# Splitting and distributing the q and k halves of a sparse-attention kernel: where GpSimd writes them, and how many transfers carry the rest

## The chip, the cores and the metric

The program runs on one core of a Trainium2 chip (trn2). The metric is the device time of one execution in microseconds (us). A core has five engines, each with an instruction stream of its own: TensorE (PE, matmuls and transposes; its weight loads are listed as PEld), VectorE (DVE), ScalarE (ACT), GpSimd (POOL) and SyncE (SP, which issues nearly all transfers here). They meet only at semaphores. The core has 16 DMA engines.

## What is computed

Three layers follow each other: attention that keeps only scores within tau of a row's maximum, a top-1 mixture of 8 experts, and a SwiGLU layer. The change lies in the attention.

```python
batch, n_heads, seq, head_dim = (2, 8, 576, 64)
def _attn_ref(q, k, v, tau):
    scores = (1.0 / np.sqrt(q.shape[-1])) * np.matmul(q, k.transpose(0, 1, 3, 2))
    thresh = np.max(scores, axis=-1, keepdims=True) - tau
    scores = np.where(scores >= thresh, scores, -1000000000.0)
    attn = np.exp(scores - np.max(scores, axis=-1, keepdims=True))
    attn = attn / (np.sum(attn, axis=-1, keepdims=True) + 1e-09)
    return np.matmul(attn, v)
def reference(...):            # x: (1152, 512), capacity 288
    x = attn_out.transpose(0, 2, 1, 3).reshape(1152, 512)
    x = _moe_ref(x, w_gate, w1, w2, capacity)   # argmax expert, relu(x w1) w2, times its gate
    return (silu(x @ w_gate2) * (x @ w_val)) @ w_out
```

## The kernel before

**Units.** The 8 heads are taken in 4 pairs (`hp`), the 576 rows of a batch as 4 blocks of 128 and a tail of 64. A pair has 9 units: 4 blocks of batch 0, 4 of batch 1, and one unit (`st` 8) for the tails of both batches. So there are 36 units, numbered 0 to 35; pair `hp` begins at unit 9 hp. In one unit and for each of the two heads (`j`), TensorE computes 128 x 576 scores (`emit_qk`, L597, tile `s`), VectorE takes the maximum (L607) and later masks (L631), ScalarE exponentiates (L620), and TensorE transposes the unit before (L653), which ScalarE copies out (L657, tile `pT`).

**Halves.** The products must be as exact as float32, so q and k are split into a rounded half and the rest (`hi`, `lo`). The tile `KP` holds for one head, on 128 partitions, both halves of k: one in partitions 0 to 63, the other in 64 to 127. The q tiles (`QH`, `QL`; buffers `qhl` for odd pairs, `ring[3]` and `ring[4]` for even ones) hold each half of q twice, in both partition halves. `QT` does the same for the tail rows of q.

**Staging.** For pair 0 the halves are made in another way. For pairs 1 to 3 `stage_tasks(hp + 1)` makes them while pair `hp` is computed; its five tasks go into the list `trq` at the end of unit `st == TST`, and up to two are taken per unit. A task transposes a 128 x 512 block of both heads on TensorE (`turn`, L515), ScalarE copies it to the scratch buffer `sraw` (L528, L530), GpSimd makes the rounded half and the rest into `ring[1]` or `ring[0]` (`parts`, L508 and L510, on all 128 partitions), and SP issues the transfers that carry each half of each head to its partitions: 4 per block of k (L537), 4 per block of q (L540), 4 for the tails of k (L559), and one unit after the pair has begun 8 for the tails of q (`qtails`, L568). Tasks run in the order k of batch 0, q of batch 0, tails, k of batch 1, q of batch 1.

**Values.** `pv_tasks` multiplies the masked weights with v in groups of two units: for each of four row chunks and both heads a matmul with a 128 x 64 weight (L675), and for the 64 tail rows one with a 64 x 64 weight (L678). A group's work waits in the list `pvq`. In each unit a loop with a budget (`credit`) takes from `pvq`, `trq` and `xl` (the 128 x 144 product that follows, L709); from `st >= UST` on, staging goes ahead of values.

**Queues.** TensorE, ScalarE, VectorE and GpSimd run in the order in which the code is written; SP's order is made by a scheduler. In the built program every SP transfer also waits on one of eight DMA semaphores that go round, so that it follows the landing of the transfer eight places ahead of it. `load_qkv` (L333, L336, L348) loads a pair's q, k and v from HBM, `late_consts` fills the token tables.

Of the kernel before, what the change touches and what calls it, by code (L numbers as in the profile page):

```python
# [10 lines left out]
F32 = mybir.dt.float32  # L11
# [11 lines left out]
def attention_moe_swiglu_kernel(  # L23
# [62 lines left out]
    TST = 4  # L86
    QST = 1
    FB = 1800
# [5 lines left out]
    UST = 5  # L94
# [222 lines left out]
    idw = ld.tile([128, KD, 128 + 2 * NE], F32, name="idw")  # L317

    def load_qkv(hp):
        h0 = 2 * hp  # L320
        r = raw[hp] = {}
        srcs = {"k": (k, 1), "q": (q, 1), "v": (v, 2)}
        for nm, (src, nb) in srcs.items():
            if hp and nm != "v":
                r[nm] = ld.tile([128, B, C4, 2, D], F32, tag=nm, name=nm, bufs=nb)
            else:
                r[nm] = ld.tile([128, B, 2, C4, D], F32, tag=nm, name=nm, bufs=nb)
            r[nm + "t"] = ld.tile([128, 2, D], F32, tag=nm + "t", name=nm + "t", bufs=nb)
# [24 lines left out]
        main("k", 1, nc.sync)  # L353
        main("q", 1, nc.sync)
        tail("q", nc.sync)
        for b in range(B):
            main("v", b, nc.sync)
        tail("v", nc.sync)
# [42 lines left out]
    QT = [ld.tile([128, 2, 2 * 128], F32R, name=f"qt{j}") for j in range(2)]  # L401
    QTH, QTL = [[QT[j][:, w] for j in range(2)] for w in range(2)]
    traw = ld.tile([128, 2, 128], F32, name="traw")
    thl = ld.tile([128, 2, 2, 128], F32R, name="thl")
    qhl = [ld.tile([128, 2, B * SM], F32R, name=f"qhl{j}") for j in range(2)]
    ready = set()

    def tr_qk_tasks(hp):
# [6 lines left out]
        def ensure(j):  # L415
            if (hp, j) not in KP:
                KP[hp, j] = qk.tile([128, B, S], F32R, tag=f"kp{j}", name=f"kp{j}")
                QH[hp, j], QL[hp, j] = qhl[j][:, 0], qhl[j][:, 1]
                if hp % 2 == 0:
                    QH[hp, j], QL[hp, j] = ring[3 + j][:, 0], ring[3 + j][:, 1]  # L420
# [14 lines left out]
        def qmain(b, j, w):  # L435
            def f():
                ps = mp.tile([128, 512], F32R, tag="m", name="ps_q")
                tr(ps, [fl(raw[hp]["qh" if w == 0 else "ql"][:, b, j, c]) for c in range(C4)])
                dst = (QH, QL)[w][hp, j][:, b * SM:(b + 1) * SM]
# [53 lines left out]
    def stage_tasks(hp):  # L493
        kx, qx = ring[1], ring[0]
# [3 lines left out]
        def ensure():  # L498
            if (hp, 0) in KP:
                return  # L500
            for j in range(2):
                KP[hp, j] = qk.tile([128, B, S], F32R, tag=f"kp{j}", name=f"kp{j}")
                QH[hp, j], QL[hp, j] = qhl[j][:, 0], qhl[j][:, 1]
                if hp % 2 == 0:
                    QH[hp, j], QL[hp, j] = ring[3 + j][:, 0], ring[3 + j][:, 1]

        def parts(dst, src):
            nc.gpsimd.tensor_scalar(out=dst[0], in0=src, scalar1=1.0, scalar2=1.0,  # L508
                                    op0=ALU.mult, op1=ALU.mult)
            nc.gpsimd.tensor_tensor(out=dst[1], in0=src, in1=f32(dst[0]), op=ALU.subtract)  # L510
# [7 lines left out]
        def main(nm, b):  # L518
            def f():
# [4 lines left out]
                x, dst = (kx, sraw[:, 1, cs]) if nm == "k" else (qx, sraw[:, 0, cs])  # L524

                def ev():
# [4 lines left out]
                    parts([x[:, i, cs] for i in range(2)], dst)  # L531
                    for j in range(2):
                        for i in range(2):
                            to, frm = slice(i * D, (i + 1) * D), slice(j * D, (j + 1) * D)
                            if nm == "k":
                                o = ST if j else 0
                                nc.sync.dma_start(f32(KP[hp, j][to, b, o:o + SM]), f32(x[frm, i, cs]))  # L537
                            else:
                                t = ring[3 + j] if hp % 2 == 0 else qhl[j]
                                nc.sync.dma_start(f32(t[to, :, cs]), f32(x[frm, :, cs]))  # L540
# [5 lines left out]
        def tails():  # L546
# [3 lines left out]
            def ev():  # L550
                nc.scalar.copy(traw[:, 0], ps[:, 0:128])
                nc.scalar.activation(out=traw[:, 1], in_=ps[:, 128:256], func=ACTF.Identity,
                                     scale=kfac[:, 0:1])
                parts([thl[:, i] for i in range(2)], traw)
                for j in range(2):
                    o = 0 if j else SM
                    frm = slice(j * D, (j + 1) * D)
                    for i in range(2):
                        nc.sync.dma_start(  # L559
                            f32(KP[hp, j][i * D:(i + 1) * D, :, o:o + ST]),  # L560
                            f32(thl[frm, i, 1]).rearrange("p (b t) -> p b t", b=B))
            return ev, None

        def qtails():
            for j in range(2):
                for i in range(2):
                    for w in range(2):
                        nc.sync.dma_start(  # L568
                            f32(QT[j][i * D:(i + 1) * D, w]).rearrange(
                                "p (x t) -> p x t", t=ST)[:, 0:4:3, :],  # L570
                            f32(thl[j * D:(j + 1) * D, w, 0]).rearrange("p (b t) -> p b t", b=B))
# [13 lines left out]
    def emit_qk(i):  # L585
# [4 lines left out]
        col = (b * C4 + c) * 128  # L590
        if b >= 0:
            jobs = [(QH[hp, j][:, col:col + 128], b), (QL[hp, j][:, col:col + 128], b)]
# [69 lines left out]
    def pv_tasks(g):  # L662
# [5 lines left out]
        def item(bb, o, w, c, last):  # L668
            def f():
# [3 lines left out]
                for j in range(2):  # L673
# [104 lines left out]
    keep_warm(mp, WARM0, 128)  # L778
    nc.scalar.dma_start(tau_sb, tau.partition_broadcast(128))
# [82 lines left out]
    for u in range(NU):  # L862
        hp, st = divmod(u, 9)
        live, tpos = u < NU, 0 <= u - 1 < NU
        if u == 5:
            late_consts()
# [70 lines left out]
        if live and hp and st == QST:  # L937
            qtails()
    assert not trq
# [134 lines left out]
    olo = [rp.tile([128, 128], BF16, name=f"olo{t}") for t in range(NTL)]  # L1074
# [482 lines left out]
```

## Time and profile before

| | us |
|---|---|
| median of 3 runs (561.7 to 566.77) | 564.54 |
| the profiled execution: its time | 564.97 |
| its span, from the first instruction to the last | 563.3 |
| attention, about | 10 to 172 |
| mean granted TensorE clock, share of full speed | 0.986 |

The page's 40 slices show TensorE busy in almost every slice, 95% of the span. That is a share over stages with different limits, and a matmul that waits inside its pipeline counts as busy, so a stage is read from the starts of its units and from the waits, which the section on the rows shows.

### The profile page before, as it was taken

Reading aid. Unit: us, or ns where it says so; the run is one execution under the profiler, and the core shown is the slowest. Engines: PE = TensorE matmul, PEld = TensorE weight load, DVE = VectorE, ACT = ScalarE, POOL = GpSimd, SP = SyncE. Lnnn points to the kernel's source line nnn. Section 1 sums busy time; section 2 is a strip of 40 time slices with the busy share of each in tenths; the row PEclk is TensorE's granted clock in tenths of the full one; section 3 lists DMA queues with packets and bytes.
Section 4 is the critical chain, followed back from the end, with each engine's and each line's share of the span. In section 5 each row is a group of like instructions: output and inputs, shape, how many; then the busy total and the mean of one; then the engine's idle time right before and its main releaser. Section 6 shows DMA issues by size and latency. Waiting matters only on the chain. (4 is left out here: it accounts for less than half of the span.)

```text
span 563.3 us, 9844 instructions
## 1 busy us (share of the span) xinstructions
PE 536.4 (95%) x3600; PEld 481.0 (85%) x3602; DVE 409.7 (73%) x825; ACT 295.2 (52%) x573; POOL 85.4 (15%) x145
## 2 busy tenths in 40 slices
PE   7999988999997799999999999999999999999996
PEld 6787866877773799998998889999999999888884
DVE  5988876888876399989988977888896748722220
ACT  4977664676651399877866743334332333332321
POOL 6541050055452500000000000000000000011101
PEclk8999998999999799999999999999999999999999
DMA  7557467457301888977666442442341300000001
GB/s 185 173 150 171 118 143 172 110 140 205 116 29 35 313 289 281 328 224 232 224 219 223 151 149 81 145 149 83 143 149 76 112 40 1 0 38 37 20 38 42
DMA packets 67895, 77.94 MB, mean 138 GB/s; under 512 B 25216, under 2 KB 43136, under 8 KB 67840
## 3 DMA queue, kind: packets, MB, share of 16 engines
q1 hardware_dynamic: 66256, 72.52, 42.4%
q0 software_dynamic: 1440, 4.72, 2.2%
q8 instruction: 30, 0.49, 0.3%
q14 instruction: 25, 0.20, 0.1%
q10 hardware_dynamic: 144, 0.00, 0.0%
HBM read 61.89 MB, written 4.72 MB: 118 GB/s over the span
## 5 line engine op out<-in xcount | busy, mean ns | idle before, releaser
L1460 PE MATMUL pgv<-yT,ring 128*128 128x384 f32 x828 | 145.1, 337 | 0.0
L1460 PEld LDWEIGHTS pgv<-yT,ring 128*128 128x128 f32 x828 | 144.9, 188 | 0.0
L210 ACT CAST ring<-raw 128x1024 fp32r<-128x1024 f32 x57 | 60.8, 1066 | 51.2 <-DVE raw L238 49.5
L657 ACT COPY pT<-ps_pt 128x512 f32<-128x512 f32 (+1 forms) x108 | 52.3, 486 | 41.6 <-PE ps_pt L653 41.6
L607 DVE TENSOR_REDUCE nm<-s 128x1 f32<-128x576 f32 x72 | 54.4, 755 | 17.2 <-PE s L597 17.1
L631 DVE SCALAR_TENSOR_TENSOR e<-s,th,e 128x576 f32<-128x576 f32 x72 | 58.7, 816 | 6.2 <-ACT e L620 4.9
L1513 POOL DMA_INDIRECT out_dram<-ob,ids x9 | 8.7, 972 | 358.9 <-ACT ob L1512 351.7
L620 ACT ACTIVATE e<-s,nm 128x576 f32<-128x576 f32 x72 | 54.3, 754 | 2.2 <-DVE nm L607 1.8
L288 DVE TENSOR_TENSOR ring<-raw,ring 128x1024 fp32r<-128x1024 f32 x44 | 53.3, 1218 | 0.0
L1231 PE MATMUL ps_y<-h,ring 128*128 128x448 f32 (+3 forms) x160 | 48.8, 370 | 3.6 <-DVE h L1358 3.4
L214 DVE TENSOR_TENSOR hs<-h,hs 128x768 fp32r<-128x768 f32 x18 | 17.2, 958 | 48.1 <-ACT hs L210 48.1
L653 PE MATMUL ps_pt<-ident,e 128*128 128x128 f32 x324 | 47.9, 276 | 0.0
L1231 PE MATMUL ps_h<-xw,ring 128*128 128x448 f32 (+3 forms) x160 | 46.4, 362 | 0.0
L1508 PE MATMUL po<-ring,hs 128*128 128x512 f32 x108 | 42.0, 389 | 0.0
L1507 PE MATMUL po<-ring,hs 128*128 128x512 f32 x108 | 42.0, 389 | 0.0
L1509 PE MATMUL po<-ring,hs 128*128 128x512 f32 x108 | 42.0, 389 | 0.0
L1232 PE MATMUL ps_y<-h,ring 128*128 128x224 f32 (+3 forms) x160 | 40.0, 250 | 0.0
L1232 PE MATMUL ps_h<-xw,ring 128*128 128x224 f32 (+3 forms) x160 | 40.0, 250 | 0.0
L675 PE MATMUL ps_pv<-pT,v 128*64 128x256 f32 (+2 forms) x400 | 39.9, 331 | 0.0
L653 PEld LDWEIGHTS ps_pt<-ident,e 128*128 128x128 f32 x324 | 39.7, 142 | 0.2 <-issue 0.2
L1231 PEld LDWEIGHTS ps_y<-h,ring 128*128 128x128 f32 x160 | 30.0, 188 | 8.3 <-DVE h L1358 7.4
L1480 ACT ACTIVATE sg<-pgv 128x384 f32<-128x384 f32 x36 | 17.5, 486 | 28.4 <-PE pgv L1460 18.9
(224 smaller groups left out, 975.9 us busy)
## 6 DMA issues: line engine op xcount, KB each, us to landing
raw<-in_moe_w_dram SPq DMA_DIRECT2D x25, 1024.0 KB, 5.1
rawx<-in_moe_w_dram SPq DMA_DIRECT2D x7, 1024.0 KB, 5.9
raw<-in_moe_w_gate_dram SPq DMA_DIRECT2D x6, 1024.0 KB, 5.0
qhl<-ring SPq DMA_DIRECT2D x16, 256.0 KB, 4.4
raw<-in_moe_w_out_dram SPq DMA_DIRECT2D x4, 1024.0 KB, 4.9
kp<-ring SPq DMA_DIRECT2D x24, 128.0 KB, 2.3
rawx<-in_moe_w_val_dram SPq DMA_DIRECT2D x3, 1024.0 KB, 5.0
raw<-in_moe_w_val_dram SPq DMA_DIRECT2D x3, 1024.0 KB, 5.0
```

What stands on the lines that cost most here:

```text
L210: nc.scalar.copy(dst, src)
L288: lo_eng.tensor_tensor(out=lo_, in0=src, in1=f32(hi_), op=ALU.subtract)
L607: nc.vector.tensor_reduce(out=nm_t[u][:, j:j + 1], in_=s_t[i][:, :, 0:SH], axis=AX.XY, op=ALU.max, negate=True)
L620: nc.scalar.activation(out=e_t[u][:, j].rearrange("p (a s) -> p a s", a=2), in_=s_t[i][:, :, 0:SH], func=ACTF.Exp, bias=nm_t[u][:, j:j + 1 ...
L631: nc.vector.scalar_tensor_tensor(out=ev, in0=s_t.pop(i)[:, :, 0:SH], scalar=th_t[u][:, j:j + 1], in1=ev, op0=ALU.is_ge, op1=ALU.mult, accu ...
L653: nc.tensor.transpose(ps[:, c * 128:(c + 1) * 128], ef[:, (c0 + c) * 128:(c0 + c + 1) * 128], ident)
L657: return lambda: nc.scalar.copy(pT[g][:, c0:c0 + m, o:o + 128], ps[:, 0:m * 128].rearrange("p (c t) -> p c t", c=m))
L1231: mm(ps[:, 0:2 * W], ws(wp, 0), x[:, 0:2 * W], start=first, stop=False)
L1232: mm(ps[:, 0:W], ws(wp, 1), x[:, 0:W], start=False, stop=last)
L1460: mm(ps[:, 0:TH], (gw, vw)[w][:, i, kk, fl * 128:(fl + 1) * 128], yT[:, x, kk, th * TH:(th + 1) * TH], start=i + x + kk == 0, stop=i == 1 ...
L1507: mm(po, hs[:, 0, fl], ws[:, 0, sl], start=f == 0, stop=False)
L1508: mm(po, hs[:, 0, fl], ws[:, 1, sl], start=False, stop=False)
```

## The change

- GpSimd writes one half of each split straight into the tile where it belongs: for k, the rounded half of head 0 into `KP` (partitions 0 to 63) and the rest of head 1 into `KP` (64 to 127); the two other halves go through `ring[1]` and one transfer each. For q both halves are written in place and one transfer per head copies them to the other partitions. Each GpSimd instruction covers 64 partitions instead of 128, so there are twice as many.
- By the order that the built programs print, a pair needs 30 SP transfers where it needed 50 (the rows of one pair, its loads and its results counted; the note on the change says 52).
- The order of tasks is k, tails, q for batch 0, then k and q of batch 1; `TST` goes from 4 to 3 and `UST` from 5 to 4.
- The tails of v lie in two fixed tiles `vtail`, zeroed at the start, one 128-row weight per head: its own 64 rows, zeros in the other 64.
- From pair 2 on v is loaded at `st == VST` (5) of the pair before, not with q and k; `late_consts` runs at unit 11, not 5; `olo` takes the space of an `e` buffer.

```diff
-    TST = 4
+    TST = 3
     QST = 1
+    VST = 5
...
-    UST = 5
+    UST = 4
...
+    vtail = [ld.tile([128, B, 2, D], F32, name=f"vtail{i}") for i in range(2)]
...
             if hp and nm != "v":
-                for h in range(2):
-                    eng.dma_start(r[nm][:, b, :, h],
-                                  srcs[nm][0][b, h0 + h, 0:SM, :].rearrange("(p c) d -> p c d", c=C4))
+                eng.dma_start(r[nm][:, b],
+                              srcs[nm][0][b, h0:h0 + 2, 0:SM, :].rearrange(
+                                  "h (p c) d -> p c h d", c=C4))
...
-                eng.dma_start(r[nm + "t"][i * ST:(i + 1) * ST], src_t)
+                dst = r[nm + "t"][i * ST:(i + 1) * ST]
+                eng.dma_start(dst[:, :, i] if nm == "v" else dst, src_t)
...
-                    parts([x[:, i, cs] for i in range(2)], dst)
-                    for j in range(2):
-                        for i in range(2):
...
-                                nc.sync.dma_start(f32(KP[hp, j][to, b, o:o + SM]), f32(x[frm, i, cs]))
...
-                                nc.sync.dma_start(f32(t[to, :, cs]), f32(x[frm, :, cs]))
+                    lo_, up = slice(0, D), slice(D, 2 * D)
+                    if nm == "k":
+                        k0, k1 = [KP[hp, j][:, b, o:o + SM] for j, o in ((0, 0), (1, ST))]
+                        x = kx[:, cs]
+                        rounded(k0[lo_], dst[lo_])
+                        rest_of(x[lo_], dst[lo_], k0[lo_])
+                        nc.sync.dma_start(f32(k0[up]), f32(x[lo_]))
+                        rounded(x[up], dst[up])
+                        rest_of(k1[up], dst[up], x[up])
+                        nc.sync.dma_start(f32(k1[lo_]), f32(x[up]))
+                    else:
+                        for j, frm, to in ((0, lo_, up), (1, up, lo_)):
+                            t = by_batch(ring[3 + j] if hp % 2 == 0 else qhl[j])[:, b]
+                            rounded(t[frm, 0:SM], dst[frm])
+                            rest_of(t[frm, SM:2 * SM], dst[frm], t[frm, 0:SM])
+                            nc.sync.dma_start(f32(t[to]), f32(t[frm]))
...
-        return [main("k", 0), main("q", 0), tails, main("k", 1), main("q", 1)], qtails
+        return [main("k", 0), tails, main("q", 0), main("k", 1), main("q", 1)], qtails
...
-                        mm(ps[j * D:(j + 1) * D, o:o + w], r["vt"][j * ST:(j + 1) * ST, bb, :],
-                           p[j * ST:(j + 1) * ST, C4, o:o + w], start=False, stop=True)
+                        mm(ps[j * D:(j + 1) * D, o:o + w], r["vt"][:, bb, j, :],
+                           p[:, C4, o:o + w], start=False, stop=True)
...
+    for vz in vtail:
+        nc.vector.memset(vz, 0.0)
...
-        if u == 5:
+        if u == 11:
             late_consts()
...
+        if live and st == VST and hp + 1 in vlate:
+            assert not any(g[0] < hp for _, _, g in pvq)
+            vlate.pop(hp + 1)()
```

The order of the built programs shows three places. SP, staging of pair 2 (during pair 1), before: the transfers of the first block of k (`kp<-ring`), of q (`ring_98`, `ring_99`), results of pair 0 (`xd<-xr`), the tails of k (`kp<-thl`), then the second block of k.

```order
L748 DMA xd<-xr 128x3x128
L537 DMA kp_1118<-ring_96 64x512 x2
L537 DMA kp_1119<-ring_96 64x512 x2
L540 DMA ring_98<-ring_95 64x2x512 x2
L540 DMA ring_99<-ring_95 64x2x512 x2
L748 DMA xd<-xr 128x128
L748 DMA xd<-xr 128x2x128
L559 DMA kp_1118<-thl 64x2x64 x2
L559 DMA kp_1119<-thl 64x2x64 x2
```

The same place of the change:

```order
L557 DMA kp_1063<-ring_96 64x512
L560 DMA kp_1064<-ring_96 64x512
L586 DMA kp_1063<-kth 64x2x64
L589 DMA kp_1064<-kth 64x2x64
L775 DMA xd<-xr 128x128
L775 DMA xd<-xr 128x2x128
L337 DMA k<-in_k_dram 128x8x64
L566 DMA ring_98<-ring_98 64x1024
L566 DMA ring_99<-ring_99 64x1024
```

The tails of k now stand third and fourth and not eleventh to fourteenth, and six transfers carry what twelve did. One load for pair 3 (`k<-in_k_dram`) now stands among them.

GpSimd, the same staging, before: the first block of k (`ring_96`), a logit sum (`lg`) in between, the first block of q (`ring_95`) and the tails (`thl`).

```order
L508 TENSOR_SCALAR ring_96<-raw_103 128x512
L510 TENSOR_TENSOR ring_96<-raw_103,ring_96 128x512
L508 TENSOR_SCALAR ring_95<-raw_103 128x512
L510 TENSOR_TENSOR ring_95<-raw_103,ring_95 128x512
L729 TENSOR_TENSOR lg<-lt 128x24
L508 TENSOR_SCALAR thl<-traw 128x256
L510 TENSOR_TENSOR thl<-traw,thl 128x256
```

The same place of the change, up to where the first block of q begins (it has four such instructions too, into `ring_98` and `ring_99`):

```order
L526 TENSOR_SCALAR kp_1063<-raw_103 64x512
L530 TENSOR_TENSOR ring_96<-raw_103,kp_1063 64x512
L526 TENSOR_SCALAR ring_96<-raw_103 64x512
L530 TENSOR_TENSOR kp_1064<-raw_103,ring_96 64x512
L526 TENSOR_SCALAR kp_1063<-traw 64x2x64
L530 TENSOR_TENSOR kth<-traw,kp_1063 64x128
L526 TENSOR_SCALAR kth<-traw 64x128
L530 TENSOR_TENSOR kp_1064<-traw,kth 64x2x64
L526 TENSOR_SCALAR thl<-traw 128x128
L530 TENSOR_TENSOR thl<-traw,thl 128x128
L756 TENSOR_TENSOR lg<-lt 128x24
```

Ahead of the last result of q's first block there were four instructions on 512 columns; now there are eight of these, and six on the tails.

TensorE, end of one unit and the next two, in pair 1, before: `ps_pv<-pT,v` are value matmuls with a 128-row weight, `ps_pv<-pT,vt` those with a 64-row weight, the rest are scores and transposes.

```order
L678 MATMUL ps_pv<-pT,vt 64x256 x2
L675 MATMUL ps_pv<-pT,v 64x64 x8
L678 MATMUL ps_pv<-pT,vt 64x64 x2
L675 MATMUL ps_pv<-pT,v 64x64 x4
L597 MATMUL s<-kp_607,qhl_127 128x288 x4
L653 MATMUL ps_pt<-ident,e 128x128 x4
L597 MATMUL s<-kp_608,qhl_128 128x288 x4
L653 MATMUL ps_pt<-ident,e 128x128 x5
L675 MATMUL ps_pv<-pT,v 64x64 x4
L678 MATMUL ps_pv<-pT,vt 64x64 x2
L675 MATMUL ps_pv<-pT,v 64x256 x6
```

The same place of the change, one unit earlier in the program (`vtail_123` is the padded weight, 128 rows):

```order
L705 MATMUL ps_pv<-pT,vtail_123 64x256 x2
L702 MATMUL ps_pv<-pT,v 64x64 x8
L705 MATMUL ps_pv<-pT,vtail_123 64x64 x2
L702 MATMUL ps_pv<-pT,v 64x64 x4
L624 MATMUL s<-kp_555,qhl_130 128x288 x4
L680 MATMUL ps_pt<-ident,e 128x128 x4
L624 MATMUL s<-kp_556,qhl_131 128x288 x4
L680 MATMUL ps_pt<-ident,e 128x128 x5
L702 MATMUL ps_pv<-pT,v 64x64 x4
L705 MATMUL ps_pv<-pT,vtail_123 64x64 x2
```

The matmuls are the same in number and columns, but all rows of values now have weights of one shape. The last row shown before, six matmuls of the next group, has moved to the unit after.

## Rows read from the trace of the kernel before

**Rows 1.** Waits of TensorE, 12 to 172 us: engine, line, releaser, total us, times, longest.
```profile
PE s L597 <- DMA kp<-thl: 3.4, 2, 3.1
```

**Rows 2.** Timeline of TensorE: start, us, line, x count; starts of units 9, 10, 18, 19, 27, 28.
```profile
44.64 0.79 PE L597 MATMUL s<-kp,qhl 128*128 128x288 f32 x4
48.90 0.81 PE L597 MATMUL s<-kp,qhl 128*128 128x288 f32 x4
...
82.55 0.53 PE L597 MATMUL s<-kp,ring 128*128 128x288 f32 x2
86.14 0.57 PE L597 MATMUL s<-kp,ring 128*128 128x288 f32 x2 [3.06 <-DMA kp<-thl]
91.72 0.80 PE L597 MATMUL s<-kp,ring 128*128 128x288 f32 x4
...
125.36 0.53 PE L597 MATMUL s<-kp,qhl 128*128 128x288 f32 x2
130.22 0.81 PE L597 MATMUL s<-kp,qhl 128*128 128x288 f32 x4
```

**Rows 3.** Busy time by stretch; columns: length, PE, PEld, DVE, ACT, POOL, PEclk, DMA.
```profile
88.00:90.00 2.00, 2.00 (x12) 1.50 (x12) 1.44 (x4) 1.47 (x4) 0.00 (x0) 0.52 0.41 95
```

**Rows 4.** Timeline of SP's queue, staging of pair 2: start, us for all, x count.
```profile
70.72 3.11 SPq L537 DMA_DIRECT2D kp<-ring  x4
...
79.73 3.23 SPq L559 DMA_DIRECT2D kp<-thl  x4
```

**Rows 5.** Timeline of GpSimd, staging of pair 2.
```profile
70.07 0.62 POOL L508 TENSOR_SCALAR ring<-raw 128x512 fp32r<-128x512 f32 x1 [3.73 <-DMA qt<-thl]
...
72.01 0.61 POOL L508 TENSOR_SCALAR ring<-raw 128x512 fp32r<-128x512 f32 x1
...
74.16 0.41 POOL L508 TENSOR_SCALAR thl<-traw 128x256 fp32r<-128x256 f32 x1
...
75.34 0.62 POOL L508 TENSOR_SCALAR ring<-raw 128x512 fp32r<-128x512 f32 x1
```

**Rows 6.** Transfers, 20 to 130 us: x count, KB each, median us to landing.
```profile
kp<-ring SPq DMA_DIRECT2D x24, 128.0 KB, 2.3
qhl<-ring SPq DMA_DIRECT2D x12, 256.0 KB, 4.4
...
kp<-thl SPq DMA_DIRECT2D x12, 32.0 KB, 2.8
```

**Rows 7.** Timeline of TensorE, blocks of value matmuls in units 9 to 11.
```profile
46.88 1.52 PE L675 MATMUL ps_pv<-pT,v 128*64 128x256 f32 x12
48.32 0.65 PE L678 MATMUL ps_pv<-pT,vt 64*64 64x256 f32 x4
...
51.15 1.95 PE L675 MATMUL ps_pv<-pT,v 128*64 128x256 f32 x16
53.03 0.79 PE L597 MATMUL s<-kp,qhl 128*128 128x288 f32 x4
...
55.26 0.65 PE L678 MATMUL ps_pv<-pT,vt 64*64 64x256 f32 x4
55.84 0.69 PE L675 MATMUL ps_pv<-pT,v 128*64 128x64 f32 x16
```

**Rows 8.** Timeline of VectorE: first maximum of units 6 and 7.
```profile
32.83 0.75 DVE L607 TENSOR_REDUCE nm<-s 128x1 f32<-128x576 f32 x1
...
36.29 0.76 DVE L607 TENSOR_REDUCE nm<-s 128x1 f32<-128x576 f32 x1
```

**Rows 9.** Timeline of TensorE: start of unit 14, which holds pair 2's first staging.
```profile
65.57 0.80 PE L597 MATMUL s<-kp,qhl 128*128 128x288 f32 x4
```

**Rows 10.** Groups of GpSimd instructions, 28 to 130 us: total, mean ns of one.
```profile
L510 POOL TENSOR_TENSOR ring<-raw,ring 128x512 fp32r<-128x512 f32 x12 | 15.3, 1278 | 1.0
```

**Rows 11.** Timeline of VectorE at the start.
```profile
4.33 0.15 DVE L785 TENSOR_SCALAR kfac<-tau_sb 128x1 f32<-128x1 f32 x1 [2.70 <-DMA tau_sb<-in_tau_dram]
```

**Rows 12.** Instructions of L678: count, ns min/median/max, first and last start, forms.
```profile
L678 PE MATMUL ps_pv<-pT,vt x100: 218/376/428, 27.5 to 170.9; 64*64 64x256 f32 x60, 64*64 64x64 f32 x32, 64*64 64x128 f32 x8
```

More of the change, by code (lines that the diff above doesn't have):

```diff
@@ L355, in load_qkv, with values @@
         tail("q", nc.sync)
-        for b in range(B):
-            main("v", b, nc.sync)
-        tail("v", nc.sync)
+        def values():
+            for b in range(B):
+                main("v", b, nc.sync)
+            tail("v", nc.sync)
+        if hp < 2:
+            values()
+        else:
+            vlate[hp] = values
+    vlate = {}
     def prep_tasks(hp, pick):
@@ L400, in attention_moe_swiglu_kernel, with by_batch, q_pair @@
     QH, QL, KP = {}, {}, {}
-    QT = [ld.tile([128, 2, 2 * 128], F32R, name=f"qt{j}") for j in range(2)]
-    QTH, QTL = [[QT[j][:, w] for j in range(2)] for w in range(2)]
+    QT = [ld.tile([128, 5 * 128], F32R, name=f"qt{j}") for j in range(2)]
+    QTH, QTL = [[QT[j][:, w * 384:w * 384 + 256] for j in range(2)] for w in range(2)]
     traw = ld.tile([128, 2, 128], F32, name="traw")
-    thl = ld.tile([128, 2, 2, 128], F32R, name="thl")
+    thl = ld.tile([128, 2, 128], F32R, name="thl")
+    kth = ld.tile([128, 128], F32R, name="kth")
     qhl = [ld.tile([128, 2, B * SM], F32R, name=f"qhl{j}") for j in range(2)]
     ready = set()
+    def by_batch(t):
+        return t[:, :, :].rearrange("p w n -> p (w n)").rearrange("p (b n) -> p b n", b=B)
+    def q_pair(hp, j):
+        t = by_batch(ring[3 + j] if hp % 2 == 0 else qhl[j])
+        return [t[:, :, w * SM:(w + 1) * SM] for w in range(2)]
     def tr_qk_tasks(hp):
@@ L502, in ensure, with rounded, rest_of @@
                 KP[hp, j] = qk.tile([128, B, S], F32R, tag=f"kp{j}", name=f"kp{j}")
[L503 to L508, printed above, removed]
+                QH[hp, j], QL[hp, j] = q_pair(hp, j)
+        def rounded(dst, src):
+            nc.gpsimd.tensor_scalar(out=dst, in0=src, scalar1=1.0, scalar2=1.0,
                                     op0=ALU.mult, op1=ALU.mult)
-            nc.gpsimd.tensor_tensor(out=dst[1], in0=src, in1=f32(dst[0]), op=ALU.subtract)
+        def rest_of(dst, src, hi):
+            nc.gpsimd.tensor_tensor(out=dst, in0=src, in1=f32(hi), op=ALU.subtract)
         def turn(blocks, name):
@@ L523, in f @@
                 cs = slice(b * SM, (b + 1) * SM)
-                x, dst = (kx, sraw[:, 1, cs]) if nm == "k" else (qx, sraw[:, 0, cs])
+                dst = sraw[:, 1 if nm == "k" else 0, cs]
                 def ev():
@@ L553, in ev @@
                                      scale=kfac[:, 0:1])
[L554 to L561, printed above, removed]
+                lo_, up = slice(0, D), slice(D, 2 * D)
+                bt = lambda ap: ap.rearrange("p (b t) -> p b t", b=B)
+                k0, k1 = [KP[hp, j][:, :, o:o + ST] for j, o in ((0, SM), (1, 0))]
+                x, src = bt(kth[:, :]), bt(traw[:, 1])
+                rounded(k0[lo_], src[lo_])
+                rest_of(x[lo_], src[lo_], k0[lo_])
+                nc.sync.dma_start(f32(k0[up]), f32(x[lo_]))
+                rounded(x[up], src[up])
+                rest_of(k1[up], src[up], x[up])
+                nc.sync.dma_start(f32(k1[lo_]), f32(x[up]))
+                rounded(thl[:, 0], traw[:, 0])
+                rest_of(thl[:, 1], traw[:, 0], thl[:, 0])
             return ev, None
         def qtails():
[L565 to L571, printed above, removed]
+            for j, frm, to in ((0, slice(0, D), slice(D, 2 * D)), (1, slice(D, 2 * D), slice(0, D))):
+                q4 = QT[j][:, :].rearrange("p (y t) -> p y t", t=ST)[:, 0:10:3]
+                x = thl[:, :, :].rearrange("p w (b t) -> p (w b) t", b=B)
+                rounded(q4[frm], f32(x[frm]))
+                nc.sync.dma_start(f32(q4[to]), f32(x[frm]))
             ready.update((hp, -1, j) for j in range(2))
-        return [main("k", 0), main("q", 0), tails, main("k", 1), main("q", 1)], qtails
+        return [main("k", 0), tails, main("q", 0), main("k", 1), main("q", 1)], qtails
     units = []
@@ L589, in emit_qk @@
         s = sp.tile([128, 2, 512], F32, tag="s", name="s")
-        col = (b * C4 + c) * 128
         if b >= 0:
-            jobs = [(QH[hp, j][:, col:col + 128], b), (QL[hp, j][:, col:col + 128], b)]
+            jobs = [(Q[hp, j][:, b, c * 128:(c + 1) * 128], b) for Q in (QH, QL)]
         else:
@@ L1072, in rhs_op @@
                         in1=tokf[:, :, i].unsqueeze(2).to_broadcast([128, NTL, NTL]), op=ALU.mult)
-    olo = [rp.tile([128, 128], BF16, name=f"olo{t}") for t in range(NTL)]
+    olo_all = ep.tile([128, 2, S], F32, tag="e", name="olo")[:, :, :].rearrange(
+        "p j s -> p (j s)").bitcast(BF16)
+    olo = [olo_all[:, t * 128:(t + 1) * 128] for t in range(NTL)]
     sq = [rp.tile([128, 128], BF16, name=f"sq{i}") for i in range(len(AOLO))]
```

18 lines of the change are left out of this document (7 added, 11 removed).

## Prediction

> **What bounds the kernel now.** I read the waits first, then TensorE's timeline unit by unit, then what stood ahead of each late thing on its own engine. Attention is a loop of 36 units whose starts TensorE marks. The waits of TensorE name one large releaser, the transfer that brings the tails of k, `kp<-thl`: 3.4 us in two waits, the longest 3.1 [rows 1]. The timeline places it. Unit 18, the first of pair 2, starts at 82.55, stops after half of its first scores and goes on at 86.14; unit 19 starts at 91.72 [rows 2]. The same unit of pair 1, with the same work, takes 44.64 to 48.90, that is 4.26 [rows 2]. So unit 18 takes 9.17, an excess of 4.91, more than the wait alone: after it TensorE, idle before, runs at a granted clock of 0.52 of full speed from 88 to 90, close to the lower of its two levels, 1.2 GHz and not 2.4 [rows 3]. Unit 27, the first of pair 3, takes 4.86, an excess of 0.60 [rows 2].
>
> Why are the tails late? GpSimd had made the halves in time: its last tail instruction ends before 75.34 [rows 5]. SP is what is late: four transfers take it 3.1 to 3.2 us, 0.8 each, and the tails' own are issued from 79.73 to 82.96 [rows 4], since eight transfers of k and q and two of results stand ahead of them. With 2.8 us from issue to landing [rows 6] they come at 85.8, and TensorE goes on at 86.14. So here the number of transfers is the price, not GpSimd.
>
> The other units do not wait, so they are worth what TensorE does in them, down to a floor: units 6 and 7 start 3.46 apart on VectorE (32.83 and 36.29), which has little else to do than their maxima and masks [rows 8]. A unit with less TensorE work than that gains nothing from losing more.
>
> **The change part by part.**
>
> *Fewer transfers, tails earlier.* Ahead of the tails now stand two transfers, not eight plus two results, and the pair's first staging needs six, not twelve. The work also begins a unit earlier. If it lands in time, both excesses go: 4.91 + 0.60 = 5.51 us.
>
> *GpSimd's double work.* Whether it lands in time is now GpSimd's matter. Before, a rounded half and its rest on 128 x 512 take 72.01 - 70.07 = 1.94 us, and on 128 x 256 take 75.34 - 74.16 = 1.18 [rows 5]. No row has 64 partitions and 512 columns. If time follows columns alone, one such pair of instructions costs 1.94; if it follows partitions too, 0.97. I take 1.94, the row with the same columns, and keep 0.97 as the other bound. The first block of k then costs 3.88, the tails three pairs on 128 columns, at most 1.18 each, so 3.54, and the first block of q 3.88: 11.3 us, at the low bound half of it. GpSimd started 4.5 us after the start of its unit (65.57 [rows 9] to 70.07 [rows 5]). So the last transfer of q is issued by 15.8 us after unit 13 starts, and lands 2.3 to 4.4 later [rows 6], at 18.1 to 20.2. The need comes five units on. By the prices below these last 4.0, 4.1, 4.0, 3.7 and 5.1, together 20.9. So it is just in time at the worst bounds and 3 us early at the middle ones. Units 4 to 8 last some 20.4, the narrowest place. In-place writes need no new wait: the buffers written belong to a pair that is over.
>
> Behind GpSimd on its queue stand logit sums and, in pair 3, weight splits, with units to spare. SP's queue gains one load in the middle of the staging, which waits for a transposition done units before.
>
> At this place a rule speaks against the change. All 12 rests ran at a mean of 1278 ns beside a VectorE that is busy most of the time [rows 10], and 1.94 holds for the pair in the timeline: I see no blocking, and take none. The Trainium skill, page "SBUF — State Buffer", section "Who interferes with whom", says that a VectorE instruction in a two-port mode and a GpSimd instruction exclude each other for a whole instruction. By that rule doubled GpSimd work could hold VectorE or be held; by the row the sum stays as it is.
>
> *Padded tails of v.* This is the part that I think is worth most beside the stall. Sixteen recorded value matmuls on 256 columns take 1.88 us to the next start (51.15 to 53.03), twelve take 1.44 (46.88 to 48.32), and four with the 64-row weight take 0.58 (55.26 to 55.84, and 48.32 to 48.90) [rows 2, 7]. From 4 to 16 that is 0.107 a matmul (12 gives 0.58 + 8 x 0.107 = 1.44), and each block has 0.15 more, whatever its length. So the price is for entering a block of another weight shape, and 12 + 4 in two shapes cost 2.02 where 16 in one cost 1.88 [rows 7]. In the printed order value matmuls stand in 63 runs of one shape before; after, with one shape, in 32. That removes 31 x 0.15 = 4.65 us of TensorE time, 1.2 of it behind unit 35, where the last values follow each other. A matmul with 128 rows streams as many columns as one with 64, so nothing is added. The bounds: nothing, if the 0.15 belongs to each accumulation's end and not to the shape, and 4.65.
>
> *Moved work.* The new order gives some units more TensorE work and others less. I priced each unit as 2.23 for scores and transposes (53.03 to 55.26 [rows 7]), 1.1 more in tail units, plus its blocks as above, with 3.5 as floor. In the new order units 4, 11, 13, 20, 22 and 33 fall below the floor, together by 2.5 us; in the old, units 5, 6, 15 and 24 by 2.0. So 0.5 of the saving is lost. Bounds 0 and 2.
>
> *At no cost.* Two zero fills of `vtail` run where VectorE waits 2.70 us for the first input [rows 11]; without that cover they would cost their own half microsecond. The late load of v is asked for at unit 14 and used from unit 18 on, for 3 us of landing. The token tables move from one unit at the floor to another. `olo`'s buffer has been free for two units.
>
> The sum: 5.51 + 4.65 - 0.5 = 9.7 us. The profiled execution took 564.97; that gives 555.3. The median of the runs shown is 0.43 lower, which gives 554.9, and I write 555.0. What follows attention hangs on its end through routing, so it moves along as a whole.
>
> **The rivals.**
>
> 1. *The shape costs nothing.* The block price stays, only the stall goes: 564.97 - 5.5 = 559.5. For it: two blocks of one shape in sequence do not occur, so the trace never shows a merged block of both. Against it: 12 + 4 against 16, the same matmuls of a group, differ by just the price.
> 2. *GpSimd is late.* A late q stops TensorE at units 9, 18 and 27, three times. At 1.5 us each, with 0.6 for the clock (a third of the 4.91 - 3.06 = 1.85 that unit 18 loses behind its wait), that returns 6.3: 561.6. It ends slower than before when each stop costs over 9.7 / 3 = 3.2, say 2.2 of waiting and 1.0 of clock. With p for a pair on 512 columns and 0.6 p for one of the tails' three, 4.5 + 5.8 p + 3.4 for landing must then reach 20.9 + 2.2, so p about 2.6 and not 1.94. With 3.5 of waiting and 1.85 each it is 571.2. For it: the margin is nothing at the worst bounds. Against it: the middle ones leave 3 us.
> 3. *The padding costs.* Two 64-row weights lie in different rows and columns of the array and could run side by side, which full-height ones can't. In the trace 100 tail matmuls are recorded, 60 on 256 columns, 8 on 128 and 32 on 64 [rows 12], at 0.107 per 256 columns 7.7 us of streaming; if half was hidden, 3.9 comes back: 564.97 - 5.5 + 3.9 = 563.4. Against it: four of them take 0.58 [rows 7], which is 4 x 0.107 + 0.15; side by side they would take 0.37. The Trainium skill, page "TensorE: Matmul & The Clock Gate", section "Why this matters for your kernels", says that small matmuls in distinct row groups run concurrently; the row shows no sign of it.
> 4. *More than that.* The floor gives way or all blocks pay: 553.
>
> **How the numbers follow.** The forecast has 0.60, from 553 to 558 by the floor's bounds and the block price. Rival 1 has 0.17, rival 2 0.13, rival 3 0.04, rival 4 0.06. A measurement of this kernel can tell about 1% from no change, 5.6 us, so faster begins at 558.9: forecast 0.59, rival 4 0.06, and 0.07 of rival 1, which lies on that line, give 0.72. Slower begins at 570.2, the far end of rival 2, 0.04. The same is the rest, 0.24. The range reaches to rival 1 and to the lower side of rival 4: 552.5 to 560.5.
>
> **What would show it.** In the profile after, TensorE has no wait on `kp` at units 9, 18 and 27, the clock stays at full speed in all of attention, and these units take 4.1. Value matmuls of 4 + 12 in one run take 1.88, not 2.02. GpSimd's instructions on 64 x 512 take 0.62 and 1.28 as on 128. Attention's last unit starts 8.5 us earlier than now. The prediction is wrong if GpSimd's instructions are slower beside VectorE, if SP waits at the load put among the staging, or if the units stay at their old length though no one waits.

## The result and the profile after

The changed kernel takes 557.67 us, the median of four executions (557.18 to 558.85); the kernel before takes 564.88 beside it. The ratio is 0.9865, 95% interval 0.9834 to 0.9897: some 7.2 us faster, where 9.7 had been forecast. The profiled execution is the slowest of the four (558.85 with a span of 557.1), and one of its stretches, named below, is not typical of the kernel.

The starts of units, in the timeline of TensorE of the changed kernel (start, us, engine, line):

```profile
44.55 0.80 PE L624 MATMUL s<-kp,qhl 128*128 128x288 f32 x4
...
48.66 0.80 PE L624 MATMUL s<-kp,qhl 128*128 128x288 f32 x4
...
82.06 0.78 PE L624 MATMUL s<-kp,ring 128*128 128x288 f32 x4
...
86.19 0.80 PE L624 MATMUL s<-kp,ring 128*128 128x288 f32 x4
...
119.55 0.79 PE L624 MATMUL s<-kp,qhl 128*128 128x288 f32 x4
...
123.69 0.80 PE L624 MATMUL s<-kp,qhl 128*128 128x288 f32 x4
```

These answer [rows 2]: units 9, 18 and 27 take 4.11, 4.13 and 4.14, and the two that took 9.17 and 4.86 have lost 5.8 together. The granted clock, 0.52 behind the stall in [rows 3], is 1.00 in every 10 us from 10 to 170. TensorE's waits in the same stretch as [rows 1] (total us, times, longest) name no `kp` and no other transfer:

```profile
PE s L624 <- DVE th L642: 2.0, 2, 1.1
PE ps_r L1069 <- DVE osb L1055: 1.6, 1, 1.6
PE ps_i L1129 <- DVE olo L1112: 1.4, 1, 1.4
PE s L624 <- DVE e L658: 1.1, 3, 0.4
PE ps_t L535 <- ACT pT L684: 0.8, 3, 0.3
PE ps_x L736 <- ACT pT L684: 0.7, 2, 0.4
```

GpSimd and SP in the staging of pair 2, timelines of both:

```profile
64.98 0.61 POOL L526 TENSOR_SCALAR kp<-raw 64x512 fp32r<-64x512 f32 x1 [3.54 <-ACT raw L548]
65.68 1.28 POOL L530 TENSOR_TENSOR ring<-raw,kp 64x512 fp32r<-64x512 f32 x1
67.04 0.62 POOL L526 TENSOR_SCALAR ring<-raw 64x512 fp32r<-64x512 f32 x1
...
69.96 0.62 SPq L586 DMA_DIRECT2D kp<-kth  x1
70.67 0.62 SPq L589 DMA_DIRECT2D kp<-kth  x1
...
73.93 2.53 SPq L566 DMA_DIRECT2D ring<-ring  x2
```

A pair of instructions on 64 x 512 takes 67.04 - 64.98 = 2.06, close to the 1.94 on 128 partitions of [rows 5]: here the time goes with columns, not partitions. The last transfer of q is issued by 76.46, which is 15.9 after unit 13 starts (60.55); 15.8 was forecast. The tails of k are issued from 69.96 to 71.29, where [rows 4] has 79.73 to 82.96.

The stretches of the two profiled executions, from the starts that the timelines show (the first `ps_r` is the first product of the sort behind attention, `ps_g` the first transposition of sorted tokens):

| stretch, us | before | after | forecast of the difference |
|---|---|---|---|
| start to unit 4 | 24.69 | 23.94 | 0 |
| unit 4 to unit 35 | 135.18 | 128.28 | -8.5 |
| unit 35 to `ps_r` | 14.73 | 13.46 | -1.2 |
| `ps_r` to the first gather's issue | 6.21 | 7.81 | 0 |
| the gather's issue to `ps_g` | 4.58 | 6.81 | 0 |
| `ps_g` to the end | 377.91 | 376.80 | 0 |

So attention and what hangs directly on it gained 8.2, and behind it 2.7 went back in this execution. The 0.75 at the start belongs to the two executions and not to the change: b_early, whose start is that of the kernel before, has 23.96. The granted clock from 8 to 10 us differs (before, then after; columns as in [rows 3]). It is part of the reason and not all of it: of 13 profiled executions (the kernel before and those of the table below), the five at 0.50 to 0.59 there reach unit 4 at 24.69 to 24.81, and the eight at 1.00 at 23.94 to 24.66.

```profile
8.00:10.00 2.00, 2.00 (x17) 2.00 (x17) 1.43 (x3) 0.76 (x3) 1.83 (x5) 0.50 0.88 238
```

```profile
8.00:10.00 2.00, 1.91 (x20) 1.72 (x19) 1.44 (x3) 1.16 (x4) 1.83 (x5) 1.00 0.79 222
```

### The profile page after: what moved, and what is told of

Its sections match the earlier page's. It is cut to its first block, busy times and chain, and to the rows that moved or that the text cites. A ratio compares the mean times of both kernels' runs of the same rounds, so it can differ in the third digit from the quotient of the medians.

```text
span 557.1 us, 9817 instructions
## 1 busy us (share of the span) xinstructions
PE 529.2 (95%) x3602; PEld 478.5 (86%) x3602; DVE 409.7 (74%) x827; ACT 295.3 (53%) x573; POOL 113.7 (20%) x187
```

## The experiments

All times are medians of fully timed executions; the kernel before took 564.2 to 565.5 beside them.

| kernel | edits | us | ratio to before, 95% |
|---|---|---|---|
| after | all | 557.7 | 0.983 to 0.990 |
| a_nopad | after, tails of v with 64 rows | 562.8 | 0.996 to 1.001 |
| a_late | after, splitting a unit later | 559.6 | 0.988 to 0.994 |
| a_tab5 | after, tables at unit 5 | 566.0 | 1.001 to 1.007 |
| a_nox | after, x not beside two staging blocks | 557.1 | 0.985 to 0.994 |
| a_wbehind | after, weight loads held | 558.7 | 0.987 to 0.994 |
| b_early | before, splitting a unit earlier | 565.7 | 1.001 to 1.005 |
| b_early11 | b_early, tables at unit 11 | 559.1 | 0.988 to 0.992 |
| b_pad2 | before, padded tails of v | 560.5 | 0.990 to 0.993 |
| b_mix | b_early11 and b_pad2 together | 555.7 | 0.982 to 0.986 |
| b_mix_wb | b_mix, weight loads held | 556.2 | 0.982 to 0.990 |
| b_mix_nox | b_mix, x as in a_nox | 556.5 | 0.982 to 0.986 |

**Is the shape of a block worth anything?** a_nopad takes the padding out of the changed kernel.

```diff
-  mm(ps[j * D:(j + 1) * D, o:o + w], r["vt"][:, bb, j, :], p[:, C4, o:o + w], ...)
+  mm(ps[j * D:(j + 1) * D, o:o + w], r["vt"][j * ST:(j + 1) * ST, bb, j, :],
+     p[j * ST:(j + 1) * ST, C4, o:o + w], ...)
```

> The changed kernel, with the value blocks' tails multiplied as before: 64 rows of weights for each head and not 128 padded ones; everything else stays. Theory (each stretch of 64-row blocks costs 0.15 us, 31 stretches more, 1.2 us of it behind unit 35): 557.7 + 4.65 = 562.3 us, units of TensorE about 0.1 longer on average, the 4 + 8 blocks of a mixed run 2.0 us and not 1.87. Rival (the shape costs nothing, all of the gain is the wait at units 18 and 27): 557.7, units as long as in the changed kernel. Rival (padding costs, since two 64-row blocks ran side by side): below 557.7. In all cases no wait for kp at units 18 and 27.

It is 5.1 slower. The sixteen value matmuls of unit 18, first with 64-row tails in a_nopad, then in the changed kernel:

```profile
86.39 0.65 PE L702 MATMUL ps_pv<-pT,v 128*64 128x256 f32 x4
86.97 0.65 PE L705 MATMUL ps_pv<-pT,vtail 64*64 64x256 f32 x4
87.55 1.08 PE L702 MATMUL ps_pv<-pT,v 128*64 128x256 f32 x8
88.56 0.67 PE L624 MATMUL s<-kp,ring 128*128 128x288 f32 x3
```

```profile
84.32 0.65 PE L702 MATMUL ps_pv<-pT,v 128*64 128x256 f32 x4
84.80 0.60 PE L705 MATMUL ps_pv<-pT,vtail 128*64 128x256 f32 x4
85.23 1.03 PE L702 MATMUL ps_pv<-pT,v 128*64 128x256 f32 x8
```

88.56 - 86.39 = 2.17 in three stretches, 86.19 - 84.32 = 1.87 in one (unit 19 begins at 86.19): 0.15 for each of the two changes of shape, as [rows 7] gave by subtraction. The Trainium skill, page "TensorEngine Tiling (Array Packing)", section "Key Properties", says that a change of tiling mode drains TensorE; the rows agree.

On the kernel before, b_pad was meant to show the same. It asked for the padded tails of pair 2 while those of pair 0, in the same fixed buffer, were still to be read, so its values, and with them the work of the sort behind it, are others (10605 instructions in the profile where the kernel before has 9844), and its 665.9 us tell nothing.

> The kernel before with padded value tails alone (and, for the space in SBUF, the 128x128 selection tiles of the sort laid into one buffer of e, as in the changed kernel). Theory: the wait of 4.91 at unit 18 and 0.60 at unit 27 stays, the stretches of 64-row blocks go: 564.9 - 4.65 = 560.2 us, 0.992 of before. Rival (the shape costs nothing): 564.9. Rival (the wait takes the gain up to unit 18): the chain of GpSimd starts from transposes that move with TensorE, so it should not; if it does, 1.5 to 2 us of the 4.65 are missing.

b_pad2 asks for them at the sixth unit of a pair.

> The kernel before with padded value tails, asked for at the sixth unit of a pair as in the changed kernel, and the selection tiles of the sort in a buffer of e; splitting, transfers and tables as before. Theory (31 stretches at 0.15 us, 3.5 of it up to unit 35 and 1.2 behind it, as a_nopad showed): 564.65 - 4.7 = 560.0, the wait at units 18 and 27 unchanged. Rival (units 18 and 27 take the gain back, as SP's queue and not TensorE sets when the tails of k land): 2 to 3 us less gain, 562 to 563, with a longer wait at unit 18. The gather of the sorted tokens: if the buffer of e delays it, it is issued 7.2 us behind the first ps_r as in the changed kernel, else 6.2 as before.

It gains 4.2. The wait at unit 18 stays, and the unit now takes 91.52 - 81.22 = 10.30, unit 27 5.80. In this execution, the slowest of its four (562.06), these two units take back 2.1 of what the padding wins elsewhere, as the second rival had it.

```profile
81.22 0.53 PE L607 MATMUL s<-kp,ring 128*128 128x288 f32 x2
84.88 0.85 PE L607 MATMUL s<-kp,ring 128*128 128x288 f32 x2 [3.13 <-DMA kp<-thl]
...
91.52 0.79 PE L607 MATMUL s<-kp,ring 128*128 128x288 f32 x4
```

**What removed the stall: fewer transfers, or an earlier start?** b_early moves only the start.

```diff
-    TST = 4
+    TST = 3
-    UST = 5
+    UST = 4
```

> The kernel before, with the splitting of the next pair's q and k put one unit earlier (TST 3, UST 4), all 52 transfers and the GpSimd work as they were. Theory A (only lateness by one unit was wrong): the k tails land 4.1 us earlier, and of the 4.91 at unit 18 about 0.8 to 1.3 stay, nothing at unit 27: 564.9 - 4.2 to 4.8 = 560.1 to 560.7 us. Theory B (the number of transfers sets it, the queue on SP is busy through the whole stretch): the wait at unit 18 stays above 3 us and the time above 563. Theory C (the wait is gone altogether): 559.4, and fewer transfers were not needed.

Theories A and C missed the time; theory B had it (above 563), but by a wait at unit 18 that is not there. No wait for `kp` was left, as theory C had it, and still the kernel was no faster: units 5 and 6 took 8.23 and 5.71 (in a_nopad, which starts as early, 4.41 and 4.13). VectorE's timeline at unit 5 tells why:

```profile
28.33 0.08 DVE L631 DVE_READ_ACCUMULATOR e<-s,th,e 128x1 f32 x1
32.78 0.17 DVE L844 TENSOR_SCALAR toki<-tok 128x9 int32<-128x9 int32 x1 [4.36 <-POOL tok L841]
```

The token tables are begun by GpSimd and finished by VectorE. In the kernel before, GpSimd had them done by 21.94 and began its first split at 32.94. In b_early they stand behind the splits that begin at 28.39, VectorE waited in its order, and maxima, exponentials and TensorE behind it. b_early11 also moves the tables (`u == 5` becomes `u == 11`):

> The kernel before with two of the changed kernel's edits: the splitting one unit earlier (TST 3, UST 4) and the token tables asked for at unit 11 and not 5. All 52 transfers and GpSimd's old halves stay. In b_early, which left the tables at unit 5, no wait for kp was left at units 18 and 27, but VectorE waited 4.4 us at unit 5 for the tables, that stood behind GpSimd's splits, and units 5 to 9 lost 5.4 against a_nopad. Theory (the tables were all that ate the gain): 565.7 - 5.4 = 560.3 us, units 18 and 27 at 4.4. Rival (without in-place writing something else comes late at unit 9, the first pair with earlier staging): above 562.5, with a wait at unit 9.

It gains 5.6, with all 50 transfers of a pair and GpSimd's old halves; units 18 and 27 take 4.43 and 4.41. a_tab5 is the reverse, the changed kernel with the tables back at unit 5.

> The changed kernel with the token tables asked for at unit 5, as before. The prediction put that edit at nothing. Theory from b_early: the tables stand behind GpSimd's splits of the first block of k, here 4.1 us of four pairs, VectorE waits 4 us or more for them at unit 5, and 5 to 7 us are lost: 563 to 565. Rival (the edit is worth nothing, as predicted): 557.7.

It is 8.3 slower than the changed kernel, more than the theory's 5 to 7. GpSimd reaches the tables after k and tails, VectorE waits, and TensorE after it:

```profile
35.43 0.46 POOL L530 TENSOR_TENSOR thl<-traw,thl 128x128 fp32r<-128x128 f32 x1
35.83 0.14 POOL L868 IOTA tok<- 128x4 int32 x1
...
36.35 0.17 DVE L873 TENSOR_SCALAR toki<-tok 128x9 int32<-128x9 int32 x1 [7.21 <-POOL tok L870]
...
38.78 1.12 PE L535 MATMUL ps_k<-ident,k 128*128 128x128 f32 x4 [6.63 <-ACT pT L684]
```

a_late keeps in-place writing and 30 transfers, but starts where the kernel before did (TST 4, UST 5).

> The changed kernel with the splitting one unit later (TST 4, UST 5, as before the change): the 30 transfers and GpSimd writing in place alone. Theory A (in place writing and fewer transfers shorten the chain by more than it was late): the last split of q ends at about 76 + 4.1 = 80.1, its copy lands 2.9 later at 83.0, and unit 18 begins at 82.1 but needs q of the first batch only; a wait of 0 to 1 us at unit 18, nothing at unit 27: 557.7 to 559. Theory B (starting one unit earlier was the main thing): a wait of 3 us or more at unit 18, 561 or more.

It is 1.95 slower, between the two theories. Units 9, 18 and 27 take 5.09, 4.79 and 5.00: their second half, which needs the other head's q, starts late each time (rows of units 9 and 18, with the transfer between them).

```profile
46.45 0.77 PE L624 MATMUL s<-kp,qhl 128*128 128x288 f32 x4 [0.74 <-DMA qhl<-qhl]
...
84.00 0.77 PE L624 MATMUL s<-kp,ring 128*128 128x288 f32 x4 [0.44 <-DVE nm L634]
...
78.82 2.54 SPq L566 DMA_DIRECT2D ring<-ring  x2
```

At unit 18 the row names VectorE's maximum of the first head, which these scores do not use; the second of the two transfers is issued 0.48 before the end of its row, at 80.9, and these take a median of 2.9 to land, which is 83.8, just ahead of 84.00.

So the new transfers without the earlier start take most of the stall away but not all of it, and the earlier start alone takes all of it. What part of a_late's gain is due to the number of transfers is not shown: its tasks also stand in the new order, tails ahead of q, and no run has that order alone.

**Three edits without the rest.** b_mix joins early start, tables and padding, with 50 transfers and the old halves.

> The kernel before with three edits: splitting one unit earlier, tables at unit 11, padded value tails; the 52 transfers and GpSimd's halves through the ring stay. Theory (these three carry all of the gain, and fewer transfers with in-place writing are not needed): 560.3 - 4.7 = 555.6 us, equal to or up to 2 below the changed kernel's 557.7, since GpSimd does half as much. Rival (fewer transfers are needed beside the padding, since TensorE arrives sooner): waits for kp or q at units 9, 18, 27, 558 or more.

555.7 us: the slowest of its four executions (556.4) is below the fastest of the changed kernel (557.2), but the two were measured beside different executions of the kernel before, and the intervals of their ratios overlap. So it is at least as fast. Unit 18 takes 4.12 in it, without a wait:

```profile
82.22 0.79 PE L607 MATMUL s<-kp,ring 128*128 128x288 f32 x4
...
86.34 0.79 PE L607 MATMUL s<-kp,ring 128*128 128x288 f32 x4
```

**Where did the rest of the forecast go?** First, into units 13 and 22, which last some 4.55 where the prediction has 4.0 for unit 13. Unit 13 in the changed kernel, and then in a_nox:

```profile
62.68 0.60 PE L535 MATMUL ps_k<-ident,k 128*128 128x128 f32 x4
63.56 0.33 PE L535 MATMUL ps_t<-ident,qt 128*128 128x128 f32 x1 [0.28 <-ACT pT L684]
...
64.36 1.00 PE L736 MATMUL ps_x<-idw,xT 128*128 128x144 f32 x6 [0.36 <-ACT pT L684]
65.11 0.78 PE L624 MATMUL s<-kp,qhl 128*128 128x288 f32 x4
```

```profile
63.45 0.60 PE L535 MATMUL ps_k<-ident,k 128*128 128x128 f32 x4
64.30 0.33 PE L535 MATMUL ps_t<-ident,qt 128*128 128x128 f32 x1 [0.25 <-ACT pT L684]
64.46 0.27 PE L535 MATMUL ps_t<-ident,kt 128*128 128x128 f32 x1
64.68 0.80 PE L624 MATMUL s<-kp,qhl 128*128 128x288 f32 x4
```

```diff
-            elif xl and nx < 1:
+            elif xl and nx < 1 and nt < 2:
```

> The changed kernel, where a unit that has turned two staging blocks takes no output projection ps_x as well, so that it comes a unit later. Units 13 and 22 last 4.56 each in the changed kernel, with k, tails and x in them and no value blocks, and TensorE waits 0.28 and 0.36 in them for the activation engine. Theory (moved work cost more than the 0.5 of the prediction, since k, tails and x share four PSUM buffers): these units fall to 3.9, x goes into a unit with room, 557.7 - 1.2 = 556.5 us. Rival (x fills the next unit by as much): 557.4 to 557.9, unit 14 as much longer as 13 is shorter.

The unit falls to 3.40, but the sum does not: unit 3 to unit 35 is 0.6 shorter and unit 35 to `ps_r` 0.7 longer (14.19, not 13.46): 18 matmuls of the projection (`ps_x`) are left for behind the start of unit 35, not 12. The time is within 0.6 of the changed kernel, which the executions do not tell apart. In b_mix the same edit does the same: units 13 and 22 at 3.42 and 3.44, unit 35 to `ps_r` 14.28 and not 13.54, no gain.

> b_mix (the kernel before with early splitting, tables at unit 11 and padded value tails) with the rule of a_nox: no output projection in a unit that has turned two staging blocks. In a_nox units 13 and 22 fell from 4.55 to 3.40, later units gave half of it back, and attention came out 0.6 shorter from unit 3 to unit 35. Theory (the same here, since the units of b_mix are as long as those of the changed kernel): units 13 and 22 at 3.4, 555.7 - 0.6 = 555.1 us. Rival (GpSimd's and SP's older, longer chain becomes late when units 13 to 17 get shorter): a wait for kp or q at unit 18, 555.7 or more.

Second, behind attention. a_wbehind holds the first two weight loads of the experts until the first sorted rows are there.

```diff
+        if WS is FAST:
+            for t in idle:
+                nc.scalar.copy(t[:, 0:1], gbuf[:, 0:1])
         for _ in range(len(idle)):
             next_raw()
```

> The changed kernel, where the first two weight loads of the experts wait until the first 128 sorted rows have landed (the activation engine copies one column of them into each weight buffer ahead of its load). In the changed kernel the first gather is issued 7.8 us behind the first ps_r and lands 5.9 later, beside the weight loads issued 0.6 behind it; before the change 6.2, 3.6 and 2.0. Theory (the gather lost its time to the weight loads): it lands in 3.6 to 4.2, TensorE's wait for raw falls from 6.9 to 5 or less, and 1 to 2 us are won, 556 to 556.7. Rival (the late stores of xd set the gather's start, and the weights that come later now are needed first): the landing falls, but the time stays at 557.7 or is up to 2 longer.

The median of three landings fell from 5.9 to 3.6, and nothing was won: the time is 558.7 where the changed kernel has 557.7 and a_nox 557.1. GpSimd's issue of the first gather and VectorE's first use of its rows, in a_wbehind and in a_nox, which does not hold the loads:

```profile
173.66 1.21 POOL L1136 DMA_INDIRECT raw<-xd,ids  x1 [2.54 <-DVE slack L1154]
...
178.16 0.71 DVE L1218 TENSOR_SCALAR raw<-raw 128x512 f32<-128x512 f32 x1 [5.24 <-ACT rawx L1198]
```

```profile
173.66 1.21 POOL L1136 DMA_INDIRECT raw<-xd,ids  x1 [2.57 <-DVE slack L1154]
...
177.66 0.49 DVE L1215 TENSOR_SCALAR raw<-raw 128x512 f32<-128x512 f32 x1 [4.50 <-DMA raw<-xd,ids]
```

Without the hold the first rows come 4.0 behind the issue: the median landing of the three is 6.3, so the second and third come later, but TensorE waits only for the first. With it VectorE also waits for the copy, 4.5 behind the issue. b_mix_wb is no faster than b_mix either (556.2 and 555.7).

> b_mix (the kernel before with early splitting, tables at unit 11 and padded value tails) with the same hold of the first two weight loads. In b_mix the gather landed 6.1 behind its issue, which stood 6.5 behind the first ps_r. Theory as for a_wbehind: the gather lands in 3.6 to 4.2 and 1 to 2 us are won: 553.7 to 554.7. Rival: 555.7 or up to 2 longer, as the weights come later.

So holding the weight loads wins nothing, and the time is not lost there. What differs in all of these kernels is the gather's start. It reads `xd`, and by all that the rows show it waits for the last two stores there: it is issued 4.1 behind the issue of the last one in the kernel before and 5.6 behind it in the changed kernel, and the two stores took 3.2 to 3.5 us to land there and 4.3 to 4.7 here. (The `slack` that the rows above name is computed behind the gather in the code.) It is issued 6.2 to 6.8 behind the first `ps_r` in the seven profiled kernels without in-place writing (before, b_early, b_early11, b_pad2, b_mix, b_mix_wb, b_mix_nox) and 7.1 to 7.8 in the six with it, which also share the merged loads, the late load of v and the order of tasks. The transfers of the changed kernel behind unit 35 (KB each, median us to landing) show stores that took 3.7 and 3.3 before:

```profile
xd<-xr SPq DMA_DIRECT2D x1, 129.0 KB, 5.0
...
xd<-xr SPq DMA_DIRECT2D x2, 32.2 KB, 4.5
```

They are issued as early and are as large. The buffer that `olo` moved to is not the cause, as b_pad2 has it too and issues at 6.2. From 171 to 173 us the DMA engines have a share of 0.00 in the changed kernel, so no other traffic was in the way at the end; why the stores land later is open. In the profiled execution of the changed kernel the first rows also came late, 179.61 - 173.49 = 6.1 behind the issue. The four others with in-place writing and no hold have 4.0 to 4.1, so that part is taken as this execution's own; why it was slow is not shown.

## Why the prediction held, and where it did not

**The stall.** 5.51 was forecast and 5.8 went from the two units in the profile. The 5.6 by which b_early11 is faster looks the same, but it holds more than the stall: its earlier start also breaks the value matmuls into 70 stretches of one shape where the kernel before has 63, and from unit 3 to `ps_r` its profile is only 154.07 - 150.01 = 4.06 shorter. The sum was right, its reason only in part: "here the number of transfers is the price, not GpSimd" is true of what made the tails late, but b_early11 shows that a start one unit earlier pays that price without saving a single transfer. a_late shows how much the 30 transfers do with the new order of tasks and the old start.

**GpSimd's double work.** The mechanism held, and the 15.8 was right to 0.1 with some luck: pairs on 512 columns took 2.06 and not 1.94, the tails 71.74 - 69.10 = 2.64 and not 3.54, and SP's own 0.5 to issue was not in the sum. The two copies of q took 5.4 and 4.1 to land, the first beyond the bound of 4.4. The second, issued at 75.98, landed 2.0 before unit 18 starts, 2.9 before the second head's scores at 83.04, which use it. A start 4 us later (a_late) overdraws the margin by 0.7 to 1.0 at each of the three places, so rival 2 exists, one unit away. The rule on shared access (page "SBUF — State Buffer", section "Who interferes with whom" of the Trainium skill) brought nothing here: from unit 4 to unit 35 GpSimd is busy 46.0 us before and 75.1 after, VectorE 112.7 and 112.4 (rows under "Moved work").

**Padding.** 4.65 forecast; 5.1, 4.2 and 3.4 measured by time (a_nopad, b_pad2, b_mix against b_early11). The profiles agree better: from unit 3 to `ps_r` padding shortens 150.62 to 145.92 (a_nopad, after) and 150.01 to 145.26 (b_early11, b_mix), by 4.7 both times. Rivals 1 and 3 fall with it. But both pairs lose 70 - 32 = 38 stretches, since the earlier start splits the value matmuls further than in the kernel before (63); 38 x 0.15 would be 5.7. So the average stretch costs 0.12, and the agreement with 4.65 is in part luck.

**Moved work.** This is the first term that was mis-sized: 0.5 against some 1.4. The prediction counts units 13 and 22 among those that fall below the floor of 3.5, while its margin for GpSimd has unit 13 at 4.0. It took 4.56: k, tails and the projection all fell into it. Busy time from unit 4 to unit 35, before and then after (columns as in [rows 3]), and the start of unit 12 after:

```profile
24.69:159.87 135.18, 130.34 (x1067) 103.69 (x1067) 112.71 (x280) 91.90 (x194) 46.01 (x55) 0.99 0.59 149
```

```profile
23.94:152.22 128.28, 125.50 (x1068) 102.80 (x1067) 112.39 (x282) 91.78 (x194) 75.10 (x101) 1.00 0.45 112
...
56.02 0.76 PE L624 MATMUL s<-kp,qhl 128*128 128x288 f32 x4 [0.90 <-DVE th L642]
```

TensorE idles 135.18 - 130.34 = 4.84 before, of which 3.43 in units 18 and 27, and 128.28 - 125.50 = 2.78 after: 1.4 more outside them. In pair 1 it is the 0.90 that it waits for VectorE's threshold at unit 12, at the floor, and the 0.28 and 0.36 of unit 13 above. That leaves 0.7 of the 1.6 missing from 8.5. It is in TensorE's busy time, which fell by 130.34 - 125.50 = 4.84; forecast were 5.51 - 3.43 = 2.08 for the work behind the stall and 3.45 for padding. a_nox shows that thinning out units 13 and 22 wins nothing in time.

**"What follows attention hangs on its end through routing, so it moves along as a whole."** This step failed. From unit 4 to `ps_r` the profile is 8.2 shorter, the time fell 7.2: about 1 us is given back between `ps_r` and the issue of the gather, which all six kernels with in-place writing issue 0.9 or more later than the kernel before. What delays it is open.

**"At no cost."** For the token tables this was right in the sum and wrong in the reason. "From one unit at the floor to another" looked at VectorE's 0.5 us of work, not at what it waits for. At unit 5 GpSimd used to have nothing ahead of the tables, and that was their cover: with the new splits ahead of them the tables at unit 5 cost 8.3 us, more than the whole gain.

**The title's edit.** Nothing in the forecast asked whether in-place writing and fewer transfers were needed beside the early start. They were not: b_mix gains 9.0 without them, close to the 9.7 of the sum, and the median of the kernel with them is 1.9 higher. Of that 0.7 is in attention by the profiles (unit 3 to `ps_r` takes 145.92 in the changed kernel and 145.26 in b_mix); the rest would be behind it. No run adds in-place writing to b_mix without the merged loads, the late load of v and the new order of tasks, so which of these costs the time is not shown.

## What to carry to other kernels

When a stage is moved earlier, look at every engine's queue at its new place for short instructions that another engine waits for: tables of 0.1 us an instruction behind 4 to 7 us of splits stopped VectorE for 4.4 and 7.2 us, and TensorE behind it. Count the stretches of one weight shape that TensorE sees, not only its matmuls, and pad the odd shape if the columns stay the same. When several edits aim at one stall, time the cheapest alone first; here two constants (`TST`, `UST`) and one moved line did what a rewrite of the transfers was made for.

## What was not expected of the hardware

No row of the kernel before had shown what half the partitions cost GpSimd: it took 0.61 and 1.28 us on 64 x 512, and 0.62 and 1.28 on 128 x 512. The same stores of 129 KB took 3.6 to 4.2 us to land in kernels without in-place writing and 4.4 to 5.0 in those with it, at the same place in the program; no run tells why. And the granted clock from 8 to 10 us after the start was 0.50 to 0.59 in five of those 13 profiled executions and 1.00 in eight, whatever the kernel: a_tab5 and a_late, which open as the changed kernel does, are among the five.
